# Sums of six second-weight slices moved to later steps, and DMA issue in program order with stores behind their data

## The chip, the cores and the metric

The kernel runs on one core of one Trainium2 chip. A core has TensorE (PE, matmuls, with weight loads shown apart as PEld), VectorE (DVE), ScalarE (ACT), GpSimd (POOL) and SyncE (SP), which here issues every DMA; 16 DMA engines serve the core. The metric is the device time of one execution in microseconds (us), as a median over runs.

## What is computed

```python
attn  = concat([softmax(scale * x @ state.T) @ state,         # per batch and head
                softmax(scale * state @ x.T) @ x], axis=2)    # 4 x 8 heads, 512 + 32 rows, 64 columns
x     = attn.transpose(0, 2, 1, 3).reshape(2176, 512)   # all tokens, 512 columns
h     = x @ w_in                                              # 512 -> 2048
x     = (maximum(h, 0) + alpha * minimum(h, 0)) @ w_out       # 2048 -> 512

P = exp(x @ w_gate - max)                                     # 8 experts
for _ in range(8):
    P /= P.sum(1, keepdims=True) + 1e-9
    P /= P.sum(0, keepdims=True) + 1e-9
    P *= N / E
out = sum over e of P[:, e:e+1] * (maximum(x @ w1[e], 0) @ w2[e])   # w1[e]: 512 x 1024, w2[e]: 1024 x 512
```

Everything is float32. Each product is made of three matmuls: an operand is split into a high part in the matmul's own format and a low part (the rest), and high by low, high by high and low by high are added up.

## The kernel before

The program has a first part (attention and the dense layer, to about 440 us) and the expert part, the function `experts`, which the change touches.

The weights of the 8 experts are cut into 32 slices (`U2 = 32`, four of 256 hidden columns for each expert). The tokens are cut into three groups, so the expert part has `NS2 = 96` steps: step s works on slice s % 32 for group s // 32. A product with the first weights is made by seven multiplications of blocks in place of eight (`quad`, with the banks x, y and z in PSUM); for this each slice's matrix of first weights needs four sums of its blocks, made on GpSimd (`weights_a`). In steps 32 to 95 the product with the second weights is made in the same way (`product`), and needs four sums of the second weights' blocks. In steps 0 to 31 the second product is made plainly (`layer2_moe`, tile `po`), without those sums.

Steps 0 to 31 therefore prepare the weights for all later ones. For a slice, the first weights (tiles `wah`, `wal`, and the sums `wsh`, `wsl`) and the second weights (`w2h`, `w2l`, and the sums, tile `wz`) are made once from the raw weights, and stored to DRAM (`keep`). From step 32 on they are loaded back (`again`) and nothing of them is worked out again. The sums of the second weights are `sums_left` on DVE (four operations of 128x256 into the tile `sumb`), a copy of each pair on ACT into the high half of `wz`, and one DVE subtraction of 128x512 for each low half: six DVE and two ACT operations for a slice, all in the step of that slice (`weights_b`). The tile `wz` has one or two homes, so the next slice's copy waits until the store of this one has read it.

What is written in which order: `experts` emits a step as seven multiplications and, in steps 1 to 32, six plain second products between them. After each it calls `slot()`, 13 times in a full step. A slot lets each lane (a queue of generators: weights, gate, sums and so on) go one yield further, and fires the entries of the list `soon` that are due. DVE, ACT and PE run their instructions in exactly this written order; for SP a scheduler chose the order. Each engine works through its own queue in order, and an instruction that waits holds all those behind it.

In steps 0 to 4 the gate is also under way: after the logits (`pg`) the eight rounds of normalization (`sinkhorn`, L449 to L464) run as a chain. In a round DVE does nine small operations (`rs`, `pr`, `cs`, `cb`), PE sums over the partitions with a matmul (`pcs`) and DVE goes on from it. The rounds are written five slots apart, and `pcs` stands in PE's queue between the multiplications.

Of the kernel before, what the change touches and what calls it, by code (L numbers as in the profile page):

```python
# [19 lines left out]
P = 128  # L20
# [24 lines left out]
def body(ctx: ExitStack, tc: tile.TileContext, xt_in, xn_in, stb, stk, wd, ws, alpha, wgate, out):  # L45
# [630 lines left out]
    def keep(u, what, tiles, i):  # L676

        for x, t in zip("hl", tiles, strict=True):
            if (u, what, x) not in kept:
                kept[u, what, x] = dram.tile([P, 7, FU], F32, tag=f"{what}{x}{u}", name=f"kept_{what}{x}{u}")  # L680
            nc.sync.dma_start(out=kept[u, what, x][:, i:i + t.shape[1], :], in_=f32(t))

    def again(u, what, tiles, i):

        for x, t in zip("hl", tiles, strict=True):
            nc.sync.dma_start(out=f32(t), in_=kept[u, what, x][:, i:i + t.shape[1], :])
# [19 lines left out]
    def weights_a(s):  # L706
# [6 lines left out]
        if s >= U2:  # L713
            again(u, "a", wa, 0)
            again(u, "a", wsum, 3)
            return
# [8 lines left out]
        keep(u, "a", wa, 0)  # L725
# [4 lines left out]
        keep(u, "a", wsum, 3)  # L730
# [4 lines left out]
    def weights_b(s):  # L735
# [8 lines left out]
        if s >= U2:  # L744
            pairs = []
            for i in range(2):
# [4 lines left out]
                pairs.append([z[:, j] for j in range(2)])  # L751
            w = [x.rearrange("p f (b c) -> p (f b) c", c=FU)[:, 0:3] for x in w]
            name_left(left2, s, w, pairs)
            again(u, "b", w, 0)
            again(u, "b", pairs[0], 3)
            again(u, "b", pairs[1], 5)
# [8 lines left out]
        keep(u, "b", [x[:, 0:1, 0:FU] for x in w], 0)  # L765
        keep(u, "b", [x[:, 1].rearrange("p (b c) -> p b c", c=FU) for x in w], 1)
# [5 lines left out]
        halves = raw.rearrange("p f (b c) -> p f b c", c=FU)  # L772
        yield from sums_left(nc.vector, sums, halves[:, 0, 0], halves[:, 1, 0], halves[:, 1, 1], halves[:, 0, 1], 1)
        load_b2(s + 1, p2["raw"])
        for i in range(2):
            if i and s >= 2 and s != U2 - 1:
                z = big.tile([P, 2, 2, FU], F32R, tag="xl3" if s < U2 - 6 else "xl5", name=f"wz_{s}_{i}")
            else:
                z = p2["z"].tile([P, 2, 2, FU], F32R, tag="z", name=f"wz_{s}_{i}", bufs=1)
# [581 lines left out]
    def experts():  # L1361
# [132 lines left out]
```

## Time and profile before

| | |
|---|---|
| three timed runs | 1876.51, 1880.92 and 1881.73 us; median 1880.92 |
| the profiled execution | 1878.26 us, span 1876.4 us |
| PE | 1793.8 us busy (96%) |
| DVE | 1495.2 us (80%) |
| POOL | 1259.6 us (67%) |
| ACT | 736.2 us (39%) |
| DMA | 424.09 MB, mean 226 GB/s |

The span is from the first to the last instruction of the program. A busy PE is a PE with a matmul in it; at half of its clock it is busy for twice as long with the same work, so its granted clock (PEclk, a share of 2.4 GHz) is read with it. In the expert part a step takes 15.6 us where nothing disturbs it in the first group, 14.6 us in the second and 12.3 us in the third.

### The profile page before, as it was taken

Reading aid. Unit: us, or ns where it says so; the run is one execution under the profiler, and the core shown is the slowest. Engines: PE = TensorE matmul, PEld = TensorE weight load, DVE = VectorE, ACT = ScalarE, POOL = GpSimd, SP = SyncE. Lnnn points to the kernel's source line nnn. Section 1 sums busy time; section 2 is a strip of 40 time slices with the busy share of each in tenths; the row PEclk is TensorE's granted clock in tenths of the full one; section 3 lists DMA queues with packets and bytes.
Section 4 is the critical chain, followed back from the end, with each engine's and each line's share of the span. In section 5 each row is a group of like instructions: output and inputs, shape, how many; then the busy total and the mean of one; then the engine's idle time right before and its main releaser. Section 6 shows DMA issues by size and latency. Waiting matters only on the chain.

```text
span 1876.4 us, 29641 instructions
## 1 busy us (share of the span) xinstructions
PE 1793.8 (96%) x10173; PEld 1667.3 (89%) x10173; DVE 1495.2 (80%) x2318; ACT 736.2 (39%) x1394; POOL 1259.6 (67%) x1297
## 2 busy tenths in 40 slices
PE   6799999988989999999999999999999999999998
PEld 5688888876778888888889999999999999999997
DVE  6744777776899998988997777777788888777886
ACT  6755666644333434333332222222223233332332
POOL 4523555465657877778756777777777898777774
PEclk8899999999999999999999999999999999999998
DMA  5111111122658888888788777777777788888882
GB/s 219 46 51 46 57 46 57 46 73 110 236 209 290 311 303 298 296 299 312 276 310 315 253 255 263 263 265 250 257 267 252 273 306 306 314 312 312 299 300 88
DMA packets 179525, 424.09 MB, mean 226 GB/s; under 512 B 20256, under 2 KB 37152, under 8 KB 179376
## 3 DMA queue, kind: packets, MB, share of 16 engines
q1 hardware_dynamic: 179376, 422.20, 63.4%
q8 instruction: 81, 1.33, 0.3%
q14 instruction: 68, 0.56, 0.1%
HBM read 299.13 MB, written 122.99 MB: 225 GB/s over the span
## 4 chain that ended last, share of the span: by engine, by line
PE 67%; DVE 6%; DMA 1%; issue 1%; ACT 0%; SPq 0%; DVEq 0%; ACTq 0%
PE pm L989 22%; PE py L816 14%; PE po L1133 11%; PE px L816 9%; PE pz L816 9%; DMA kept_bl<-wz 1%; DVE g2l L839 1%; DVE wz L784 1%; DVE oa L1151 0%; DVE c L823 0%; PE pe L1065 0%; DVE u L823 0%; DVE m L995 0%; DMA wsl<-kept_al 0%; DVE oa L1155 0%
## 5 line engine op out<-in xcount | busy, mean ns | idle before, releaser
L995 DVE TENSOR_TENSOR m<-pm,m 128x768 f32<-128x768 f32 (+1 forms) x427 | 378.0, 887 | 124.1 <-PE pm L989 124.1
L989 PE MATMUL pm<-formgh,wz 128*128 128x384 f32 (+1 forms) x1134 | 212.6, 322 | 0.3 <-DVE m L995 0.3
L920 POOL TENSOR_TENSOR formgh<-mid,formgh 128x384 fp32r<-128x384 f32 (+1 forms) x126 | 121.4, 964 | 107.9 <-ACT formgh L919 107.8
L816 PE MATMUL py<-rT,wsh 128*128 128x384 f32 (+1 forms) x768 | 189.3, 329 | 1.8 <-DVE u L823 1.7
L816 PE MATMUL px<-rB,wah 128*128 128x384 f32 (+1 forms) x768 | 189.2, 329 | 1.1 <-DVE g2l L839 1.0
L989 PEld LDWEIGHTS pm<-formgh,wz 128*128 128x128 f32 x1134 | 186.7, 188 | 0.6 <-issue 0.6
L536 POOL TENSOR_TENSOR gl<-r,gh 128x512 fp32r<-128x512 f32 (+1 forms) x80 | 94.4, 1192 | 114.8 <-ACT gh L535 60.2
L838 ACT ACTIVATE g2h<-c 128x384 fp32r<-128x384 f32 x96 | 50.5, 526 | 301.9 <-DVE c L823 301.9
L672 POOL TENSOR_TENSOR w2l<-rw,w2h 128x512 fp32r<-128x512 f32 x64 | 86.0, 1366 | 115.9 <-ACT w2h L670 95.8
L1133 PE MATMUL po<-w2l,g2h 128*128 128x512 f32 x384 | 153.4, 399 | 0.0
L1133 PE MATMUL po<-w2h,g2l 128*128 128x512 f32 x384 | 150.8, 393 | 2.6 <-DVE g2l L839 2.6
L1133 PE MATMUL po<-w2h,g2h 128*128 128x512 f32 x384 | 152.5, 397 | 0.0
L816 PEld LDWEIGHTS px<-rB,wah 128*128 128x128 f32 x768 | 136.7, 189 | 7.9 <-DVE g2l L839 1.8
L816 PEld LDWEIGHTS py<-rT,wsh 128*128 128x128 f32 x768 | 136.8, 190 | 6.0 <-DVE u L823 2.6
L930 POOL TENSOR_TENSOR T<-mid,mid 128x384 f32<-128x384 f32 (+1 forms) x126 | 118.3, 963 | 31.2 <-DVE mid L904 30.8
L1155 DVE SCALAR_TENSOR_TENSOR oa<-po,pr,oa 128x512 f32<-128x512 f32 x168 | 124.4, 741 | 16.9 <-PE po L1133 16.2
L919 ACT ACTIVATE formgh<-mid 128x384 fp32r<-128x384 f32 (+1 forms) x126 | 63.0, 500 | 177.8 <-DVE mid L904 131.0
L551 PE MATMUL po<-gl,wh 128*128 128x512 f32 (+1 forms) x320 | 120.1, 376 | 13.0 <-DVE acc L568 11.2
L904 DVE SCALAR_TENSOR_TENSOR mid<-mid,pb 128x384 f32<-128x384 f32 (+1 forms) x192 | 121.9, 635 | 6.6
L816 PE MATMUL py<-rT,wsl 128*128 128x384 f32 (+1 forms) x384 | 125.7, 327 | 0.0
L816 PE MATMUL px<-rB,wal 128*128 128x384 f32 (+1 forms) x384 | 125.6, 327 | 0.0
L823 DVE TENSOR_TENSOR u<-py,p 128x384 f32<-128x384 f32 (+1 forms) x192 | 102.3, 533 | 28.4 <-PE py L816 16.7
(255 smaller groups left out, 5187.7 us busy)
## 6 DMA issues: line engine op xcount, KB each, us to landing
wsh<-kept_ah SPq DMA_DIRECT2D x64, 512.0 KB, 4.0
wsl<-kept_al SPq DMA_DIRECT2D x64, 512.0 KB, 5.2
wz<-kept_bh SPq DMA_DIRECT2D x126, 256.0 KB, 5.9
wz<-kept_bl SPq DMA_DIRECT2D x126, 256.0 KB, 5.9
wah<-kept_ah SPq DMA_DIRECT2D x64, 384.0 KB, 3.0
wal<-kept_al SPq DMA_DIRECT2D x64, 384.0 KB, 3.7
w2h<-kept_bh SPq DMA_DIRECT2D x63, 384.0 KB, 5.8
w2l<-kept_bl SPq DMA_DIRECT2D x63, 384.0 KB, 6.6
```

The lines of the kernel that those rows point to most:

```text
L536: nc.gpsimd.tensor_tensor(out=lo, in0=r, in1=f32(hi), op=ALU.subtract)
L551: nc.tensor.matmul(ps, lhsT=w2(wt, u, f, d * P, P), rhs=g[:, f, :n], start=(i == 0), stop=(i == 3 * NF - 1))
L672: nc.gpsimd.tensor_tensor(out=lo[:, i], in0=src[:, i], in1=f32(hi[:, i]), op=ALU.subtract)
L816: nc.tensor.matmul(bank[b], lhsT=w[:, k * P:(k + 1) * P], rhs=xf[:, j, k, :], start=(first and i == 0), stop=(i == 5), skip_group_check=True,)
L823: nc.vector.tensor_tensor(out=out, in0=bank[b], in1=t[x], op=ALU.add)
L904: nc.vector.scalar_tensor_tensor(out=out, in0=src, scalar=0.0, in1=pb[:, e % 2, h * n:(h + 1) * n], op0=ALU.max, op1=ALU.mult)
L920: nc.gpsimd.tensor_tensor(out=lo, in0=out, in1=f32(hi), op=ALU.subtract)
L930: nc.gpsimd.tensor_tensor(out=out, in0=x, in1=y, op=ALU.subtract)
L989: nc.tensor.matmul(ps[:, q, :n], lhsT=w[:, q * P:(q + 1) * P], rhs=x, start=(j == 0), stop=(j == 2))
L995: nc.vector.tensor_tensor(out=mm[g][name], in0=ps[:, :, :n], in1=mm[g][name], op=ALU.add)
L1133: nc.tensor.matmul(ps, lhsT=x[:, f, t * P:(t + 1) * P], rhs=w[:, f, :], start=(i == 0), stop=(i == 3 * NF - 1))
L1155: nc.vector.scalar_tensor_tensor(out=a, in0=ps, scalar=p, in1=a, op0=ALU.mult, op1=ALU.add)
```

## The change

Five things are edited.

1. The sums of the second weights are taken out of the steps of slices 0, 1, 2, 3, 4 and 31 (`APART`). A new lane, `apart`, which starts in step 6, loads these six raw slices a second time, one after the other, and makes their sums then, in homes of their own (`rwl` in xh4, `sumb` in xl4, `wz` in xl5). A slice takes 34 slots: the additions stand at slots 0, 2, 3 and 5, the copies of ACT at 6 and 20 and the subtractions of DVE at 7 and 21. The first addition stands at slot 16 from the start of step 6, which is in step 7, and the last subtraction in step 21.
2. In the steps of these six slices the next raw slice is loaded one slot after the split and not after the sums.
3. `keep` no longer issues a store at once: it puts it on `soon`, to be written into the program three slots later.
4. The kept tensors are cut by what is stored together, so that each is one DMA: the high and low half of a `wz` are one store and one load of 512 KB, where they were two of 256 KB.
5. SP joins the engines whose order is the written order (`manual_schedule`) in the expert part, and the load of the routing weights `pb` is written in the middle of a step and not ahead of it.

The instructions of PE are the same, in the same order. DVE and ACT have the same instructions apart from those that are moved; there are six loads more (3 MB).

```diff
-    def keep(u, what, tiles, i):
-        for x, t in zip("hl", tiles, strict=True):
...
-            nc.sync.dma_start(out=kept[u, what, x][:, i:i + t.shape[1], :], in_=f32(t))
+    def keep(key, i, n, src):
+        if key not in kept:
...
+        soon.append([3, lambda: nc.sync.dma_start(out=kept[key][:, i:i + src.shape[1], :], in_=f32(src))])
+    def again(key, t):
+        nc.sync.dma_start(out=f32(t), in_=kept[key])
...
+        if s in APART:
+            load_b2(s + 1, p2["raw"])
+            yield 1
+            return
         yield 2
-        if s < 2:
-            sums = p2["t"].tile([P, 4, FU], F32, tag="y", name=f"sumb{s}", bufs=1)
...
+        yield from sums_b(u, raw, "xh5", 1, 0)
+
+    def sums_b(u, raw, home, gap, rest):
+        sums = big.tile([P, 4, FU], F32, tag=home, name=f"sumb{u}")
+        halves = raw.rearrange("p f (b c) -> p f b c", c=FU)
+        yield from sums_left(
+            nc.vector, sums, halves[:, 0, 0], halves[:, 1, 0], halves[:, 1, 1], halves[:, 0, 1], gap
+        )
+        if not rest:
+            load_b2(u + 1, p2["raw"])
         else:
-            sums = big.tile([P, 4, FU], F32, tag="xh5", name=f"sumb{s}")
...
+            load_apart(u)
         for i in range(2):
...
             nc.scalar.activation(out=hi, in_=src, func=AF.Copy)
             yield 1
             nc.vector.tensor_tensor(out=lo, in0=src, in1=f32(hi), op=ALU.subtract)
-            keep(u, "b", (hi, lo), 3 + 2 * i)
-            yield 1
+            keep(("bs", i, u), 0, 4, z.rearrange("p x b c -> p (x b) c"))
+            yield 1 + rest
+
+    APART = [0, 1, 2, 3, 4, U2 - 1]
...
+    def load_apart(u):
+        i = APART.index(u) + 1 if u is not None else 0
+        if i < len(APART):
+            v = APART[i]
+            raw_apart[v] = big.tile([P, NF, DM], F32, tag="xh4", name=f"rwl_{v}")
+            nc.sync.dma_start(out=raw_apart[v], in_=ws[v, 1].rearrange("p (f c) -> p f c", f=NF))
+
+    def apart():
+        load_apart(None)
+        yield 16
+        for u in APART:
+            yield from sums_b(u, raw_apart[u], "xl4", 2, 12)
...
+            if s == UE + 2:
+                lanes["apart"].append(apart())
...
+            if s == U2 - 6:
+                flush("apart")
...
-        with tc.manual_schedule(engines={mybir.EngineType.DVE}):
+        with tc.manual_schedule(engines={mybir.EngineType.DVE, mybir.EngineType.SP}):
             experts()
```

What stands in DVE's queue between step 0 and step 1, before the change (`c` and `g2l` are the results of step 0's multiplications, `u` the first add of step 1):

```order
L823 TENSOR_TENSOR c_0_4183<-pz_4069,u_0_4053 128x384
L695 TENSOR_TENSOR sumb_4197<-rw_0_4006 128x256
L698 TENSOR_TENSOR sumb_4197<-sumb_4197,rw_0_4006 128x256
L700 TENSOR_TENSOR sumb_4197<-rw_0_4006 128x256
L703 TENSOR_TENSOR sumb_4197<-rw_0_4006,sumb_4197 128x256
L784 TENSOR_TENSOR wz_0_4204<-sumb_4197,wz_0_4204 128x512
L784 TENSOR_TENSOR wz_1_4209<-sumb_4197,wz_1_4209 128x512
L823 TENSOR_TENSOR u_1_4239<-py_4232,p_1_4223 128x384
L839 SCALAR_TENSOR_TENSOR g2l_4015<-c_0_4104,g2h_4014 128x384
L839 SCALAR_TENSOR_TENSOR g2l_4015<-px_4016,g2h_4014 128x384
```

And after it:

```order
L857 TENSOR_TENSOR c_0_4183<-pz_4069,u_0_4055 128x384
L857 TENSOR_TENSOR u_1_4222<-py_4215,p_1_4206 128x384
L873 SCALAR_TENSOR_TENSOR g2l_4017<-c_0_4104,g2h_4016 128x384
L873 SCALAR_TENSOR_TENSOR g2l_4017<-px_4018,g2h_4016 128x384
L873 SCALAR_TENSOR_TENSOR g2l_4017<-c_0_4154,g2h_4016 128x384
```

The six operations on slice 0 are gone from between `c` and `u`.

DVE's queue in step 7 after the change (`rw_7` is that step's own raw slice, `rwl` the raw slice 0 that is loaded again):

```order
L693 TENSOR_TENSOR sumb_5370<-rw_7_5254 128x256
L696 TENSOR_TENSOR sumb_5370<-sumb_5370,rw_7_5254 128x256
L693 TENSOR_TENSOR sumb_5383<-rwl_5169 128x256
L1189 SCALAR_TENSOR_TENSOR oa_4288<-po_6_1_5385,pr,oa_4288 128x512
L698 TENSOR_TENSOR sumb_5370<-rw_7_5254 128x256
L857 TENSOR_TENSOR u_7_5413<-py_5345,p_7_5328 128x384
L857 TENSOR_TENSOR c_7_5415<-pz_5372,u_7_5413 128x384
L701 TENSOR_TENSOR sumb_5370<-rw_7_5254,sumb_5370 128x256
L696 TENSOR_TENSOR sumb_5383<-sumb_5383,rwl_5169 128x256
L1189 SCALAR_TENSOR_TENSOR oa_4288<-po_6_2_5422,pr,oa_4288 128x512
L873 SCALAR_TENSOR_TENSOR g2l_5320<-c_7_5415,g2h_5319 128x384
L698 TENSOR_TENSOR sumb_5383<-rwl_5169 128x256
```

The rows with `rwl` are new in this step; all others stood there before in the same order.

SP's queue for the stores of one step and the loads for the next, before:

```order
L681 DMA kept_ah_5247<-wah_5216 128x768
L681 DMA kept_al_5249<-wal_5217 128x768
L681 DMA kept_ah_5247<-wsh_5218 128x1024
L681 DMA kept_al_5249<-wsl_5219 128x1024
L665 DMA rw_7_5313<-in_ws_dram 128x1024
L681 DMA kept_bh_5228<-wz_0_5315 128x512
L681 DMA kept_bl_5230<-wz_0_5315 128x512
```

And after:

```order
L681 DMA kept_a_h_5184<-wah_5155 128x768
L681 DMA kept_a_l_5185<-wal_5156 128x768
L665 DMA rw_7_5254<-in_ws_dram 128x1024
L681 DMA kept_as_h_5224<-wsh_5157 128x1024
L681 DMA kept_as_l_5225<-wsl_5158 128x1024
L681 DMA kept_bs_6_5266<-wz_0_5256 128x1024
```

The load of the next raw slice (L665) now stands ahead of the two stores of `wsh` and `wsl`, and a `wz` is stored by one DMA.

## Rows read from the trace of the kernel before

**Rows 1.** Busy time by stretch: PE, PEld, DVE, ACT, POOL, then PEclk, DMA share, GB/s.
```profile
440.21:491.50 51.29, 43.53 (x227) 35.97 (x226) 32.56 (x63) 20.21 (x36) 24.06 (x28) 0.93 0.51 190
491.50:548.80 57.30, 45.25 (x208) 38.31 (x207) 54.81 (x123) 15.81 (x29) 34.91 (x40) 0.94 0.68 243
569.60:866.80 297.20, 297.20 (x1488) 266.54 (x1488) 271.75 (x404) 120.17 (x215) 234.50 (x247) 1.00 0.84 299
900.00:962.80 62.80, 62.77 (x314) 56.10 (x313) 62.56 (x92) 24.62 (x44) 46.08 (x48) 1.00 0.80 291
962.80:997.20 34.40, 31.30 (x152) 26.80 (x151) 30.16 (x43) 11.94 (x20) 11.52 (x9) 1.00 0.88 317
1466.50:1839.30 372.80, 372.80 (x2547) 372.29 (x2546) 304.70 (x482) 115.25 (x246) 296.98 (x338) 1.00 0.85 303
```

**Rows 2.** Waits at 440.21 to 548.8 us: total us, times, longest us.
```profile
ACT wz L782 <- DMA kept_bl<-wz: 11.4, 2, 6.1
...
PE pcs L459 <- DVE cs L456: 11.1, 5, 3.8
...
PE pz L816 <- DVE g2l L839: 7.6, 1, 7.6
```

**Rows 3.** Order of time on DVE around 460 us; idle before it in brackets.
```profile
458.48 1.75 DVE L784 TENSOR_TENSOR wz<-sumb,wz 128x512 fp32r<-128x512 f32 x1
463.88 0.69 DVE L784 TENSOR_TENSOR wz<-sumb,wz 128x512 fp32r<-128x512 f32 x1 [3.65 <-ACT wz L782]
464.49 0.55 DVE L823 TENSOR_TENSOR u<-py,p 128x384 f32<-128x384 f32 x1
...
466.24 1.61 DVE L839 SCALAR_TENSOR_TENSOR g2l<-c,g2h 128x384 fp32r<-128x384 f32 x2
```

**Rows 4.** DVE groups at 491.5 to 548.8 us: busy us, mean ns of one.
```profile
L784 DVE TENSOR_TENSOR wz<-sumb,wz 128x512 fp32r<-128x512 f32 x6 | 5.3, 886 | 0.0
...
L695 DVE TENSOR_TENSOR sumb<-rw 128x256 f32<-128x256 f32 x3 | 2.0, 670 | 0.0
...
L698 DVE TENSOR_TENSOR sumb<-sumb,rw 128x256 f32<-128x256 f32 x3 | 3.1, 1029 | 0.1
...
L700 DVE TENSOR_TENSOR sumb<-rw 128x256 f32<-128x256 f32 x3 | 1.7, 579 | 0.0
...
L703 DVE TENSOR_TENSOR sumb<-rw,sumb 128x256 f32<-128x256 f32 x3 | 1.6, 537 | 0.0
```

**Rows 5.** The same groups at 569.6 to 866.8 us, 19 steps.
```profile
L784 DVE TENSOR_TENSOR wz<-sumb,wz 128x512 fp32r<-128x512 f32 x38 | 44.6, 1174 | 0.0
...
L698 DVE TENSOR_TENSOR sumb<-sumb,rw 128x256 f32<-128x256 f32 x19 | 20.7, 1087 | 0.7
...
L695 DVE TENSOR_TENSOR sumb<-rw 128x256 f32<-128x256 f32 x19 | 18.4, 970 | 0.0
...
L700 DVE TENSOR_TENSOR sumb<-rw 128x256 f32<-128x256 f32 x19 | 18.1, 953 | 0.0
...
L703 DVE TENSOR_TENSOR sumb<-rw,sumb 128x256 f32<-128x256 f32 x19 | 11.5, 603 | 0.0
```

**Rows 6.** Order of time: one operation with GpSimd idle, one with it at work.
```profile
456.36 0.42 DVE L698 TENSOR_TENSOR sumb<-sumb,rw 128x256 f32<-128x256 f32 x1
...
695.01 2.55 POOL L672 TENSOR_TENSOR w2l<-rw,w2h 128x512 fp32r<-128x512 f32 x2 [3.19 <-DMA kept_bh<-wz]
...
696.59 1.25 DVE L695 TENSOR_TENSOR sumb<-rw 128x256 f32<-128x256 f32 x1
```

**Rows 7.** Order of time on ACT in step 31.
```profile
979.83 0.63 ACT L782 ACTIVATE wz<-sumb 128x512 fp32r<-128x512 f32 x1 [3.88 <-DMA kept_bl<-wz]
```

**Rows 8.** A load's issue, the operation that reads it, its usual time to landing.
```profile
704.01 0.71 SPq L665 DMA_DIRECT2D rw<-in_ws_dram  x1
...
709.52 1.05 ACT L670 ACTIVATE w2h<-rw 128x1024 fp32r<-128x1024 f32 x1
...
rw<-in_ws_dram SPq DMA_DIRECT2D x19, 512.0 KB, 4.7
```

More of the change, by code (lines that the diff above doesn't have):

```diff
@@ L674, in body @@
     kept = {}
[L676 to L686 removed]
+    def keep(key, i, n, src):
+        if key not in kept:
+            name = "kept_" + "_".join(map(str, key))
+            kept[key] = dram.tile([P, n, FU], F32, tag=name, name=name)
+        soon.append([3, lambda: nc.sync.dma_start(out=kept[key][:, i:i + src.shape[1], :], in_=f32(src))])
+    def again(key, t):
+        nc.sync.dma_start(out=f32(t), in_=kept[key])
     def name_left(into, s, base, pairs):
@@ L713, in weights_a @@
         if s >= U2:
-            again(u, "a", wa, 0)
-            again(u, "a", wsum, 3)
+            for x, w, t in zip("hl", wa, wsum, strict=True):
+                again(("a", x, u), w)
+                again(("as", x, u), t)
             return
@@ L724, in weights_a @@
         split2(*wa, t[:, 0:3, :])
-        keep(u, "a", wa, 0)
+        for x, w in zip("hl", wa, strict=True):
+            keep(("a", x, u), 0, 3, w)
         yield next(make) + 1
@@ L729, in weights_a @@
         split2(*pairs[1], sums[:, 2:4, :])
-        keep(u, "a", wsum, 3)
+        for x, w in zip("hl", wsum, strict=True):
+            keep(("as", x, u), 0, 4, w)
         if "raw" in p2:
@@ L764, in weights_b @@
                 nc.sync.dma_start(out=whole[x], in_=f32(t))
-        keep(u, "b", [x[:, 0:1, 0:FU] for x in w], 0)
-        keep(u, "b", [x[:, 1].rearrange("p (b c) -> p b c", c=FU) for x in w], 1)
-        yield 2
-        if s < 2:
-            sums = p2["t"].tile([P, 4, FU], F32, tag="y", name=f"sumb{s}", bufs=1)
-        else:
-            sums = big.tile([P, 4, FU], F32, tag="xh5", name=f"sumb{s}")
-        halves = raw.rearrange("p f (b c) -> p f b c", c=FU)
-        yield from sums_left(nc.vector, sums, halves[:, 0, 0], halves[:, 1, 0], halves[:, 1, 1], halves[:, 0, 1], 1)
-        load_b2(s + 1, p2["raw"])
+        for x, t in zip("hl", w, strict=True):
+            keep(("b", x, u), 0, 3, t[:, 0:1, 0:FU])
+            keep(("b", x, u), 1, 3, t[:, 1].rearrange("p (b c) -> p b c", c=FU))
+        if s in APART:
+            load_b2(s + 1, p2["raw"])
+            yield 1
+            return
+        yield 2
+        yield from sums_b(u, raw, "xh5", 1, 0)
[7 more added lines that the diff above has]
+            load_b2(u + 1, p2["raw"])
+        else:
+            load_apart(u)
         for i in range(2):
-            if i and s >= 2 and s != U2 - 1:
-                z = big.tile([P, 2, 2, FU], F32R, tag="xl3" if s < U2 - 6 else "xl5", name=f"wz_{s}_{i}")
+            if rest:
+                z = big.tile([P, 2, 2, FU], F32R, tag="xl5", name=f"wz_{u}_{i}")
+            elif i:
+                z = big.tile([P, 2, 2, FU], F32R, tag="xl3" if u < U2 - 6 else "xl5", name=f"wz_{u}_{i}")
             else:
-                z = p2["z"].tile([P, 2, 2, FU], F32R, tag="z", name=f"wz_{s}_{i}", bufs=1)
+                z = p2["z"].tile([P, 2, 2, FU], F32R, tag="z", name=f"wz_{u}_{i}", bufs=1)
             hi, lo = z[:, 0], z[:, 1]
@@ L1178, in body @@
     made = {}
-    later, soon, lanes = [], [], {"x": [], "state": [], "gate": [], "early": [], "sums": [], "blocks": [], "v": [], "w": [], "w2": [], "h": [], "out": []}
+    later, soon, lanes = [], [], {"x": [], "state": [], "gate": [], "early": [], "sums": [], "blocks": [], "v": [], "w": [], "w2": [], "apart": [], "h": [], "out": []}
     wait = dict.fromkeys(lanes, 0)
```

19 lines of the change are left out of this document (11 added, 8 removed).

## The prediction

> **What bounds the kernel now.** I read the busy time by stretch first. In steps 6 to 24 (569.60 to 866.80 us) PE is busy for all of 297.20 us, and in 30 steps of the third group (1466.50 to 1839.30 us) for all of 372.80 us; both run at a granted clock of 1.00, the upper level of 2.4 GHz [rows 1]. PE's instructions stay the same in the same order, so these two stretches can only lose. Time can come back only where PE has holes, and the same view shows three such stretches: 440.21 to 491.50 us (steps 0 to 2), 491.50 to 548.80 us (the eight rounds of normalization) and 962.80 to 997.20 us (steps 31 and 32). PE is busy there for 43.53 of 51.29, 45.25 of 57.30 and 31.30 of 34.40 us [rows 1]. These are the steps that lose their own sums.
>
> The waits tell who is late. In the first stretch PE waits once, for 7.6 us, for DVE's `g2l`; ACT's `wz` copy has waited 11.4 us in two goes for the store of the `wz` before it [rows 2]. DVE in order of time shows the link: the second subtraction of slice 0 starts only at 463.88, after 3.65 us in which DVE waited for that copy, and `u` and the `g2l` that PE wants are queued right behind it [rows 3]. So store, copy, subtraction, `g2l` and PE form one chain. In the second stretch PE waits for the small operations of the rounds (`pcs` for `cs`, 11.1 us in five goes) [rows 2], and DVE is busy for 54.81 of 57.30 us [rows 1]: the rounds are late because DVE is full.
>
> **Steps 0 to 2.** The change takes the six operations out from between `c` and `u`. What is left is PE's own work. The granted clock of 0.93 means that about 0.14 of 51.29 us, 7.2 us, ran at the lower level of 1.2 GHz (the two levels average to 0.93); at the upper level this work takes half, 3.6 us less. So PE needs 43.53 - 3.6 = 39.9 us, and 51.29 - 39.9 = 11.4 could go. I take off 1 us for hand-offs which were hidden behind the wait: **10.4**. The low bound is 6.8, if the clock stays as it was (51.29 - 43.53 = 7.8, less the same 1).
>
> **The normalization.** Three slices lie in this stretch, and their sums take DVE 5.3 + 2.0 + 3.1 + 1.7 + 1.6 = 13.7 us [rows 4]. Without them DVE needs 54.81 - 13.7 = 41.1. PE needs 45.25 less half of the time at the lower clock (0.94, so 0.12 x 57.30 = 6.9, half is 3.4): 41.8. The two come out almost level, so neither hides the other's hand-offs; each of the eight rounds passes from DVE to PE and back, and I put 0.4 us on each, 3 us, by choice. 41.8 + 3 = 44.8, a gain of **12.5**. Bounds: 15.5 with no such loss, and 4 if the chain of a round, and not DVE's fullness, sets its pace (then about a third of the 11.1 us of `pcs` waits goes).
>
> **Steps 31 and 32.** In step 31 ACT's copy waited 3.88 us for a store [rows 7]. Slice 31's sums go, PE needs its 31.30 us at full clock, and 34.40 - 31.30 = **3.1** comes back; at least 1, if a load of step 32 is late next.
>
> **Where the work goes.** The new lane puts 6 x 6 = 36 operations on DVE, 24 additions and 12 subtractions, into steps 7 to 21: 15 steps. PE has no hole there, so all depends on DVE's room. DVE is busy for 271.75 of 297.20 us over 19 steps [rows 1], so it is idle for 25.45 / 19 = 1.34 us in a step and 20.1 us in 15 steps. Another stretch shows that this room can be used up: at 900.00 to 962.80 us DVE is busy for 62.56 of 62.80 us and PE loses nothing [rows 1].
>
> The price of one operation is what the trace leaves open. With GpSimd idle, a 128x256 addition took 0.42 us; another began while GpSimd was in two `w2l` subtractions and took 1.25 us, ending near the end of these [rows 6]. A 128x512 subtraction took 1.75 us and 0.69 us [rows 3]. This gives three prices for a slice. All uncontended: 4 x 0.42 + 2 x 0.69 = 3.06, so 18.4 us for six slices, inside the 20.1 us of room: cost nothing. The means of the normalization stretch: 0.670 + 1.029 + 0.579 + 0.537 + 2 x 0.886 = 4.59 [rows 4], so 27.5, an excess of 7.4. The means of steps 6 to 24: 1.087 + 0.970 + 0.953 + 0.603 + 2 x 1.174 = 5.96 [rows 5], so 35.8, an excess of 15.7. GpSimd is busy for 234.50 of 297.20 us, 79% [rows 1], and by their slots I count 25 of the 36 operations beside its work: 25/36 x 35.8 + 11/36 x 18.4 = 30.5, an excess of 10.4. Some of it stays a backlog which steps 22 and 23, without a moved slice, take up (2 x 1.34 = 2.7, say 2.4 of it). I take **8** as the cost, with 0 and 15.7 as bounds.
>
> The Trainium skill ("SBUF — State Buffer", section "Who interferes with whom") says that a VectorE instruction with two inputs in SBUF and a GpSimd instruction that reads SBUF hold one shared port as an exclusive lock, and that the loser blocks for the whole instruction. The addition of 1.25 us beside the one of 0.42 us agrees with it [rows 6]. By that rule taken to its end, every moved operation waits out one whole GpSimd instruction.
>
> **What I cost at nothing.** ACT's twelve moved copies: ACT is busy for 120.17 of 297.20 us [rows 1]. DMA: six loads and six slices' stores move into or are added to steps 7 to 21. Their traffic goes from 299 GB/s x 297.20 us / 19 = 4.68 MB in a step to about 5.28 (0.5 MB read and 1 MB stored again for 6 slices, 9 MB over 15 steps), so the DMA share of 0.84 goes to about 0.95 (an estimate in proportion). The next raw load is issued at 704.01, its first reader runs at 709.52, and such a load takes 4.7 us: 5.5 - 4.7 = 0.8 us to spare [rows 8]. The written order issues it ahead of the `wsh` and `wsl` stores, which were ahead of it, and so covers a slower transfer; were the cover gone, it would cost up to 1 us a step. Stores written three slots later meet data that are ready, so SP stands less, and only homes that wait for a store come free later; the moved sums have homes of their own. In the third group a step's loads will stand together near its start; at the DMA share of 0.85 [rows 1] they fill about 0.85 x 372.80 / 30 = 10.6 us of a step's 12.4, and the next step needs them, the sums not before its third multiplication.
>
> **Sum.** 1878.26 - 10.4 - 12.5 - 3.1 + 8 = 1860.3 for the profiled execution. The median of the three runs is 1880.92, 2.7 above it, so the forecast is **1862 us**.
>
> **Rivals**, as the median. (a) The moved operations are nearly free: then all 26 to 30 us come back, 1851 to 1855. For it speaks that two operations of six in a slice stand where GpSimd rests; against it the means in rows 5, which already are those of these steps. (b) DVE becomes the bound in steps 7 to 21 at those means: 26.0 - 15.7 = 10.3 saved, 1871. PE then has holes behind `c`, `u` and `g2l`. For it speaks a DVE that is 91% busy (271.75 of 297.20). (c) The rounds are a chain whatever else DVE does: 26.0 - 12.5 + 4 - 8 = 9.5 saved, 1871. Against it: DVE has next to no idle time in that stretch. (d) The fuller queue makes the raw load late in each of the 15 steps by 1 us: 1862 + 15 = 1877, no measurable change. (e) Slower: DVE's additions and subtractions wait for GpSimd at every turn. It decides the sign where the moved operations take more than 26.0 + 20.1 = 46.1 us together (1.28 us each), and it is measurably slower from 51.7 us (1.44 each). At the highest prices that I show, 24 x 1.25 + 12 x 1.75 = 51.0 [rows 3, 6], an excess of 30.9: 1881 - 26.0 + 30.9 = 1886, the edge of it. If each waited for two operations of GpSimd together (2.55) half of the time, 36 x 1.28 + 18.4 = 64.5, an excess of 44.4 and 1899. Against it: the means in rows 5 are far below, at 0.60 to 1.17 us. The rule of the Trainium skill named above leads to the latter number, and the trace bears it out for single operations only.
>
> **How the numbers follow.** About 0.3%, 5.6 us, is what a measurement of this kernel can tell from no change, so "same" is 1875 to 1887. The chances: the forecast (1856 to 1870) 0.55; (a) 0.13; (b) 0.09; (c) 0.06; (d) 0.08; (e) 0.09. Faster is the forecast with (a), (b) and (c): 0.83. Same is (d) and 0.02 of (e), whose price may fall near 46 us: 0.10. Slower is the rest of (e): 0.07. The range from **1850 to 1877 us** holds all cases but (e) and half of (d), 0.13 left out. Its low end is all gains at no cost (11.4 + 15.5 + 3.1 = 30.0 saved, 1851); its high end is the low bounds of the first and third gain at the highest price of rows 5 (6.8 + 12.5 + 1 - 15.7 = 4.6 saved, 1876).
>
> **What would show it.** After the change PE's hole before 466 us is gone, and ACT has no `wz` wait for a store in steps 0 to 4 and 31. The 108.6 us of the first two stretches become about 86, at a granted clock near 1.00, and `pcs` waits fall from 11.1 to 3 us or less. Steps 31 and 32 take 31.3 us. In steps 7 to 21 DVE is 98% busy or more, PE has small holes which sum to about 8 us and end at `c`, `u` or `g2l`; the moved additions show a mean near 0.8 us. PE stays full at 1466 to 1839 us. The prediction is wrong if the holes in steps 7 to 21 sum to over 16 us, if they end at `w2h` or another operation that waits for a load (then the DMA queue, and not DVE, is the price), if the rounds keep their pace, or if later steps wait for loads.

## The result, and the profile after

The changed kernel takes 1863.28 us (median of four runs, 1858.33 to 1865.91), the kernel before 1878.72 us beside it: a ratio of 0.9912, with a 95% interval of 0.9894 to 0.9929. So it is 0.9% faster; the forecast was 1862 us.

PE's records are the same 10173 in the same order in both traces, so each stretch of before can be found again in the trace after by its first and last PE instruction. The busy time by stretch after the change, for steps 0 to 2, the normalization, steps 6 to 24, steps 31 and 32, and the long stretch of the third group, as in [rows 1]:

```profile
440.30:482.60 42.30, 41.56 (x227) 34.44 (x226) 28.54 (x53) 18.42 (x33) 29.07 (x33) 1.00 0.56 199
482.60:528.20 45.60, 41.27 (x207) 35.96 (x206) 42.55 (x103) 12.39 (x22) 27.05 (x34) 1.00 0.57 208
549.20:854.80 305.60, 300.32 (x1487) 265.55 (x1486) 300.69 (x439) 123.56 (x226) 233.66 (x247) 1.00 0.90 324
951.20:981.60 30.40, 30.40 (x153) 27.24 (x152) 25.40 (x37) 10.90 (x18) 11.26 (x9) 1.00 0.91 334
1450.90:1825.70 374.80, 373.25 (x2547) 372.24 (x2545) 305.85 (x482) 114.96 (x246) 296.30 (x338) 1.00 0.83 304
```

The first two stretches are down from 51.29 and 57.30 us to 42.30 and 45.60, and PE's clock there is at its upper level all the time (1.00, where it was 0.93 and 0.94). Steps 31 and 32 went from 34.40 to 30.40 us. The price stands in the third row: 305.60 us for the 297.20 of before, with DVE busy for 300.69 of them. PE's holes there are 5.28 us; the other 3 us of the loss stand in PE's busy time, 300.32 us for 297.20 with the same instructions at the same clock, so a PE that waits is in part counted as busy. The last row holds a loss that the prediction did not have: 374.80 us for 372.80.

PE's waits for the rounds and for `g2l` at 440.3 to 552 us, beside those of [rows 2] (total us, times, longest us):

```profile
PE pcs L459 <- DVE cs L456: 4.3, 3, 2.6
...
PE pz L850 <- DVE g2l L873: 0.6, 1, 0.6
```

The `pcs` waits are down from 11.1 to 4.3 us (3 or less was expected), and the one of 7.6 us for `g2l` to 0.6. The copy `wz` no longer waits here, since it is not made here. The new waits, in steps 6 to 24 (weight loads, PEld, shown apart from matmuls):

```profile
PEld px L850 <- DVE g2l L873: 5.4, 6, 1.6
...
PEld py L850 <- DVE u L857: 3.4, 4, 1.7
PE px L850 <- DVE g2l L873: 2.9, 4, 1.1
...
PE py L850 <- DVE u L857: 1.9, 3, 1.2
```

They end where the prediction said they would, at DVE's `g2l` and `u`. No PE wait ends at a load.

The ledger below is worked out so: for each pair of PE instructions that bound a stretch, the time between them in the run's trace less the time between the same two in the trace of before. The part of the program ahead of the expert part is the same in all kernels and differs by up to 9 us between profiled executions, so it stays out. Three more parts are left out: the stretch between the normalization and step 6 (-0.8 to +0.6 us, and -2.4 with only wsh, wsl late), the second group (0.1 us at most either way) and the end of the program behind the third group's stretch (0.1 to 1.7 us less than before, and 4.0 less with the scheduler's SP order). Each row is read from one execution, so a difference of 1 or 2 us between two rows can be chance. Times and ratios are from timed runs, each ratio beside runs of the kernel before on the same chip. The names in the first column are explained with the experiments.

| run | median, us | ratio to before, 95% interval | steps 0-2 | normalization | steps 6-24 | steps 25-30 | steps 31-32 | third group |
|---|---|---|---|---|---|---|---|---|
| the change | 1863.3 | 0.9912 (0.9894 to 0.9929) | -9.0 | -11.7 | +8.6 | +0.4 | -4.1 | +2.1 |
| nothing moved | 1875.4 | 0.9979 (0.9968 to 0.9990) | -1.5 | -2.7 | 0.0 | -0.9 | +1.4 | +0.8 |
| moved, no DVE work | 1858.1 | 0.9879 (0.9862 to 0.9896) | -9.0 | -11.1 | 0.0 | -0.4 | -4.1 | +3.7 |
| moving alone | 1923.8 | 1.0232 (1.0216 to 1.0248) | -9.0 | -11.1 | +56.5 | +13.4 | -4.1 | 0.0 |
| stores at once | 1941.6 | 1.0326 (1.0310 to 1.0341) | -8.1 | -9.8 | +58.8 | +23.0 | -2.6 | +1.1 |
| spread | 1861.0 | 0.9894 (0.9873 to 0.9915) | -9.0 | -11.2 | +7.8 | -1.3 | -4.1 | +3.5 |
| quiet place | 1857.2 | 0.9868 (0.9846 to 0.9891) | -9.0 | -11.6 | 0.0 | -0.5 | -4.1 | +2.1 |
| joined alone | 1875.6 | 0.9978 (0.9963 to 0.9994) | -1.6 | -3.4 | 0.0 | -1.1 | +0.1 | 0.0 |
| scheduler's SP order | 1858.2 | 0.9870 (0.9849 to 0.9892) | -9.0 | -11.6 | +5.6 | -1.6 | -4.1 | +0.4 |
| quiet place, scheduler's SP order | 1852.1 | 0.9844 (0.9817 to 0.9870) | -9.0 | -11.4 | 0.0 | -1.7 | -4.1 | 0.0 |
| only wsh, wsl late | 1860.2 | 0.9874 (0.9849 to 0.9900) | -9.0 | -10.6 | +7.0 | -0.5 | -4.1 | +2.0 |
| loud place | 1870.1 | 0.9941 (0.9918 to 0.9964) | -9.0 | -11.7 | +13.7 | +2.5 | -4.1 | +0.7 |
| joined, homes of before | 1883.7 | 1.0009 (0.9996 to 1.0022) | +2.5 | 0.0 | 0.0 | -0.9 | +2.8 | +0.1 |

### The profile page after: what moved, and what is told of

Its sections match the earlier page's. It is cut to its first block, busy times and chain, and to the rows that moved or that the text cites. A ratio compares the mean times of both kernels' runs of the same rounds, so it can differ in the third digit from the quotient of the medians.

```text
span 1862.5 us, 29291 instructions
## 1 busy us (share of the span) xinstructions
PE 1791.9 (96%) x10173; PEld 1662.6 (89%) x10173; DVE 1507.0 (81%) x2318; ACT 732.8 (39%) x1394; POOL 1252.4 (67%) x1297
## 4 chain that ended last, share of the span: by engine, by line
PE 69%; DVE 16%; POOL 4%; issue 4%; DMA 3%; ACT 3%; SPq 1%; DVEq 0%; POOLq 0%; ACTq 0%
PE pm L1023 22%; PE py L850 11%; PE px L850 8%; PE pz L850 8%; PE po L551 7%; PE po L1167 5%; PE ph L522 4%; DVE oa L1189 2%; DVE wz L800 2%; DVE g2l L873 1%; POOL w2l L672 1%; DMA kept_bs<-wz 1%; PE pv L484 1%; DVE c L857 1%; DMA rw<-in_ws_dram 1%
## 5 line engine op out<-in xcount | busy, mean ns | idle before, releaser
L1023 PE MATMUL pm<-formgl,w2h 128*128 128x384 f32 (+1 forms) x504 | 121.2, 323 | 3.4 <-DVE m L1029 1.9
```

The source lines that it names most:

```text
L1023: nc.tensor.matmul(ps[:, q, :n], lhsT=w[:, q * P:(q + 1) * P], rhs=x, start=(j == 0), stop=(j == 2))
```

## The experiments

### What the lost time in steps 6 to 24 is made of

**Moved, no DVE work.** The lane loads and stores as before, but DVE does nothing in it; ACT copies both halves of each `wz` from the raw slice, for the two halves i of it 14 slots apart:

```diff
+    def bare_b(u, raw):
...
+            nc.scalar.activation(out=z[:, 0], in_=src, func=AF.Copy)
+            yield 1
+            nc.scalar.activation(out=z[:, 1], in_=src, func=AF.Copy)
+            keep(("bs", i, u), 0, 4, z.rearrange("p x b c -> p (x b) c"))
...
-            yield from sums_b(u, raw_apart[u], "xl4", 2, 12)
+            yield from bare_b(u, raw_apart[u])
```

> The new lane does everything but its DVE work: the raw slices are loaded again, ACT makes both halves of each wz as copies of the raw slice, and the stores are as they were. So the sums of six slices of the second weights are left out, and all of the DMA traffic stays. Theory (the lost 8.6 us of steps 7 to 21 are DVE's fullness): 1863.3 - 8.6 = 1854.7 us, PE without holes at 586 to 824 us. Rival (the loss is the DMA queue's, fuller by 3 MB and the moved stores): no gain, 1862 to 1864 us, with PE's holes still there and behind operations that wait for a load.

It took 1858.1 us, and the ledger shows 0.0 in steps 6 to 24 in place of 8.6, while the gains of the other stretches stayed. The whole price is DVE's; the six loads and the stores cost nothing there. The time came out 3 us above the 1854.7 expected. Of this the third group is 1.6 us (3.7 lost for 2.1) and the stretches from the normalization to step 6 are 1.0; the rest is not explained.

**Spread.** A slice takes 39 slots, so that the operations lie in 18 steps:

```diff
-            yield 1 + rest
+            yield 1 + rest + (1 if rest and i else 0)
...
-            yield from sums_b(u, raw_apart[u], "xl4", 2, 12)
+            yield from sums_b(u, raw_apart[u], "xl4", 2, 14)
```

> The same 36 operations on DVE, a slice in 39 slots in place of 34, so that they lie in 18 steps (7 to 24) and not in 15. Theory (DVE's room is what is short): three steps more give 3 x 1.34 = 4.0 us more of it, the loss of 8.6 us becomes about 4.6, and the time 1859 us for 1863. Rival (each moved operation that meets GpSimd's work costs PE by itself, however much room there is): the loss stays, 1863 us.

The loss was 7.8 us, and not 4.6: the theory as it stood failed in its number. The time, 1861.0 us, lies between those of the theory and its rival and decides nothing.

**Quiet place.** Two operations in each of the same 18 steps, between the last `g2l` of a step and the first `u` of the next (`low` is the subtraction of a half, `high` its copy on ACT, `make` the four additions):

```diff
-        yield 16
+        yield 12
...
         for u in APART:
-            yield from sums_b(u, raw_apart[u], "xl4", 2, 12)
+            if last:
+                low(*last)
+            yield 1
...
+            next(make)
+            yield 12
+            next(make)
+            yield 1
+            next(make)
+            yield 10
+            last = high(u, 0, sums)
+            yield 2
+            next(make)
+            load_apart(u)
+            yield 1
+            low(*last)
+            yield 10
+            last = high(u, 1, sums)
+            yield 2
+        low(*last)
```

> The same 36 operations in the same 18 steps, two in each, written between the last g2l of a step and the first u of the next, where GpSimd has nothing to do for about 3 us of each step. Theory (an operation is dear because GpSimd works beside it): 3.06 us for a slice, 18.4 us in all for 18 x 1.34 = 24.1 us of room, so the loss of 8.6 us goes and the time is 1855 us; the moved additions take 0.45 us and the moved subtractions 0.7 us. Rival (the room alone counts): as with the operations spread over 18 steps, 1859 us.

It took 1857.2 us, between the 1855 of the theory and the 1859 of the rival; the prices and the ledger decide, below.

**Loud place.** The quiet place's kernel, with the lane begun six slots later:

```diff
-        yield 12
+        yield 18
...
         for u in APART:
```

> The same pattern as at the quiet place, two operations in each of 18 steps, but six slots later, in the middle of GpSimd's work. Theory (GpSimd's work beside them makes them dear): the moved additions take 0.8 to 1.2 us and the subtractions 1.1 us or more, as a slice 5.3 to 6 us, so 32 to 36 us for 24.1 us of room, and 8 to 12 us are lost in steps 7 to 24: 1863 to 1867 us. Rival (it was the even spread of two in each step that made them free): 1857 us, as at the quiet place.

It took 1870.1 us, above the 1863 to 1867 expected: the moved operations took 37.4 us and not 32 to 36, and 2.5 us more went in steps 25 to 30.

The moved operations at the quiet place (busy us, mean ns of one; L827 are the moved subtractions):

```profile
L827 DVE TENSOR_TENSOR wz<-sumb,wz 128x512 fp32r<-128x512 f32 x12 | 8.2, 685 | 0.0
L693 DVE TENSOR_TENSOR sumb<-rwl 128x256 f32<-128x256 f32 x6 | 2.5, 424 | 0.2
L701 DVE TENSOR_TENSOR sumb<-rwl,sumb 128x256 f32<-128x256 f32 x6 | 2.5, 419 | 0.0
L698 DVE TENSOR_TENSOR sumb<-rwl 128x256 f32<-128x256 f32 x6 | 2.5, 418 | 0.0
L696 DVE TENSOR_TENSOR sumb<-sumb,rwl 128x256 f32<-128x256 f32 x6 | 2.5, 418 | 0.0
```

And at the loud place:

```profile
L827 DVE TENSOR_TENSOR wz<-sumb,wz 128x512 fp32r<-128x512 f32 x12 | 14.4, 1203 | 0.2 <-ACT wz L823 0.2
...
L696 DVE TENSOR_TENSOR sumb<-sumb,rwl 128x256 f32<-128x256 f32 x6 | 5.8, 962 | 0.0
L701 DVE TENSOR_TENSOR sumb<-rwl,sumb 128x256 f32<-128x256 f32 x6 | 5.8, 959 | 0.0
L698 DVE TENSOR_TENSOR sumb<-rwl 128x256 f32<-128x256 f32 x6 | 5.7, 956 | 0.0
L693 DVE TENSOR_TENSOR sumb<-rwl 128x256 f32<-128x256 f32 x6 | 5.7, 956 | 0.0
```

Nothing but the place differs, and the prices are 0.42 and 0.69 us at the one, 0.96 and 1.20 us at the other. In steps 6 to 24 this is 0.0 us lost against 13.7.

The place could stand for something other than GpSimd. ACT it is not: at the quiet place ACT works all through each of the 24 additions, and at the loud place all through 12 of them and not at all beside the other 12, which take 0.96 us either way. GpSimd's part can be read for each operation, here one of the loud place and one of the changed kernel (start, us):

```profile
638.01 0.93 POOL L693 TENSOR_TENSOR sum<-rw 128x256 f32<-128x256 f32 x1
...
638.27 0.95 DVE L698 TENSOR_TENSOR sumb<-rwl 128x256 f32<-128x256 f32 x1
```

```profile
578.55 0.73 POOL L701 TENSOR_TENSOR sum<-rw,sum 128x256 f32<-128x256 f32 x1
...
578.94 0.62 DVE L701 TENSOR_TENSOR sumb<-rwl,sumb 128x256 f32<-128x256 f32 x1
```

GpSimd's instructions end at 638.94 and 579.28, the additions beside them 0.28 us later, at 639.22 and 579.56. So it is with all 65 moved additions of the changed kernel, the spread and the loud run that began while a GpSimd instruction ran: each ended 0.28 to 0.29 us after that instruction. The 31 of the changed kernel and the quiet place that began with GpSimd idle took 0.41 to 0.43 us. So the price of an addition is what is left of one GpSimd instruction, and 0.28 us.

PE at the quiet place, in the stretch of steps 6 to 24:

```profile
553.50:850.60 297.10, 297.10 (x1488) 266.50 (x1487) 284.96 (x439) 125.58 (x226) 231.33 (x247) 1.00 0.90 330
```

It is busy for all of 297.10 us, as before the change, and DVE for 284.96.

Do these prices and the room of 1.34 us in a step give the losses? Loud: 5.8 + 5.8 + 5.7 + 5.7 + 14.4 = 37.4 us, less 18 x 1.34 = 24.1, is 13.3 (13.7 measured, with 2.5 more by step 30). Quiet: 10.0 + 8.2 = 18.2, which fits in 24.1 (0.0). In the changed kernel the additions take (at 564 to 810 us):

```profile
L698 DVE TENSOR_TENSOR sumb<-rwl 128x256 f32<-128x256 f32 x6 | 5.6, 932 | 0.0
L701 DVE TENSOR_TENSOR sumb<-rwl,sumb 128x256 f32<-128x256 f32 x6 | 4.7, 786 | 0.0
L693 DVE TENSOR_TENSOR sumb<-rwl 128x256 f32<-128x256 f32 x6 | 4.7, 777 | 0.0
L696 DVE TENSOR_TENSOR sumb<-sumb,rwl 128x256 f32<-128x256 f32 x6 | 4.2, 705 | 0.0
```

These are 19.2 us. The twelve subtractions share a line with those of the steps' own slices; told apart by their place in DVE's written order they take 0.67 to 1.38 us, 11.9 in all. That is 31.1 us, less 20.1 of room 11.0, of which 8.6 showed; steps 22 to 24 have room for up to 4.0. In the spread run the additions took 21.0 us (0.96 for three of the four) and the subtractions 0.67 to 0.69 each, 8.2: 29.2 in all, less 24.1, is 5.1, and 7.8 were lost. There the sum doesn't come out. It leaves out that moved operations push the steps' own ones into other places. The spread run has for two of the steps' own additions (at 554 to 850 us, 19 steps):

```profile
L696 DVE TENSOR_TENSOR sumb<-sumb,rw 128x256 f32<-128x256 f32 x19 | 26.6, 1400 | 0.6
L693 DVE TENSOR_TENSOR sumb<-rw 128x256 f32<-128x256 f32 x19 | 23.9, 1260 | 0.0
```

Before it was 20.7 and 18.4 us for the same two [rows 5]. So the runs show what makes a moved operation dear, and that at the price with GpSimd idle it costs nothing; by which rule the price turns into lost time they leave open. The rival of the spread run stands: beyond the 18.2 us of the quiet place the operations took 12.9 us in the change, 11.0 in the spread and 19.2 in the loud run, and 8.6, 7.8 and 13.7 were lost, 0.67 to 0.71 of it each time, whatever the room.

The Trainium skill ("SBUF — State Buffer", section "Who interferes with whom") has VectorE with two SBUF inputs and a GpSimd instruction that reads SBUF exclude each other for a whole instruction. The traces agree: an addition that meets a GpSimd instruction ends only behind it. They don't bear out the worst case that the prediction drew from it (64.5 us for the 36 operations, with a whole instruction of 1.28 us waited out by each); the loud place comes to 37.4, where an addition met the last 0.67 to 0.68 us of an instruction.

### What the written order and the later stores do

**Moving alone** undoes edit 3 and SP's part of edit 5, and keeps the joined transfers:

```diff
-        with tc.manual_schedule(engines={mybir.EngineType.DVE, mybir.EngineType.SP}):
+        with tc.manual_schedule(engines={mybir.EngineType.DVE}):
...
-        soon.append([3, lambda: nc.sync.dma_start(out=kept[key][:, i:i + src.shape[1], :], in_=f32(src))])
+        nc.sync.dma_start(out=kept[key][:, i:i + src.shape[1], :], in_=f32(src))
```

> The moving alone: SP's order is again the scheduler's choice, and stores are issued at once; the joined transfers stay. Theory: the written order is worth nothing in the first group, so 1863 us as with the whole change, or 1861 if the hole of 1.5 us at 1594 us, where an output store stood behind eight loads, goes with it. Rival (the order by the scheduler puts stores ahead of loads, and the moved sums need the written order): 1870 us or more, with DVE or GpSimd waiting for raw loads in steps 7 to 21.

**Stores at once** undoes edit 3 alone (the second pair of lines above).

> SP keeps the written order, but a store is written where its data are written, and not three slots later, so SP stands at every store until its data are there, and the loads behind it stand too. Theory (SP's standing is hidden, as the prediction priced it at nothing): 1863 us. Rival (the raw loads have 0.8 us to spare, and lose 1 us or more in each of some 25 steps): 1885 us or more, with GpSimd and ACT waiting for raw loads.

Both rivals were right by far: 1923.8 and 1941.6 us, slower than the kernel before. The gains of steps 0 to 5 are there in both, and 56 to 59 us go in steps 6 to 24, 3 us a step, and 13 to 23 more by step 30. The waits of the moving alone at 620 to 870 us:

```profile
POOL sum L693 <- DMA rw<-in_ws_dram: 86.0, 13, 7.5
ACT w2h L670 <- DMA rw<-in_ws_dram: 68.1, 13, 6.9
DVE sumb L693 <- DMA rw<-in_ws_dram: 40.3, 12, 4.8
```

GpSimd waits 6.6 us for the raw loads, 13 times in 250 us. SP in order of time over one such step (L656 to L665 are the four raw loads):

```profile
691.07 0.32 SPq L681 DMA_DIRECT2D kept_as_l<-wsl  x1
...
710.26 0.32 SPq L681 DMA_DIRECT2D kept_as_l<-wsl  x1
710.63 0.42 SPq L656 DMA_DIRECT2D rw<-in_ws_dram  x1
711.11 0.72 SPq L657 DMA_DIRECT2D rw<-in_ws_dram  x1
711.87 0.47 SPq L658 DMA_DIRECT2D rw<-in_ws_dram  x1
712.39 0.45 SPq L665 DMA_DIRECT2D rw<-in_ws_dram  x1
```

GpSimd and ACT in the same step:

```profile
706.33 3.90 POOL L672 TENSOR_TENSOR wsl<-sum,wsh 128x256 fp32r<-128x256 f32 x4
717.50 0.74 POOL L693 TENSOR_TENSOR sum<-rw 128x256 f32<-128x256 f32 x1 [7.26 <-DMA rw<-in_ws_dram]
```

```profile
718.60 1.06 ACT L670 ACTIVATE w2h<-rw 128x1024 fp32r<-128x1024 f32 x1 [4.25 <-DMA rw<-in_ws_dram]
```

This is a ring. GpSimd makes `wsl` until 710.2; SP has stood for that and issues the store at 710.26, and only then the four loads that it has behind it (710.63 to 712.39); GpSimd's next step begins when they are in, at 717.50, and ACT's at 718.60. Once around takes 710.26 - 691.07 = 19.2 us, against 15.6 for PE's work. In the kernel before the three small loads stood ahead of the next step's stores (691.69 to 693.49 us there), and only L665 behind the `wsl` store, with its 0.8 us to spare [rows 8]. So they stand in the run with joined transfers alone too (below); with the moved sums in the program the scheduler put all four behind. The Trainium skill ("DMA: Bandwidth & Descriptors", section "Anatomy of one DMA — SWDGE (gpsimd) path") says, of DMA engines in general, that a wait on a semaphore is held by the sequencer that issues the DMA. SP's standing here agrees with that: the four loads go out in the 2.6 us right behind the store. That the stores of `wsh` and `wsl` are what holds them is tested next.

**Only wsh, wsl late** tests the ring: the written order with stores at once, but for two stores of a step:

```diff
         soon.append([3, lambda: nc.sync.dma_start(out=kept[key][:, i:i + src.shape[1], :], in_=f32(src))])
+        if key[0] != "as":
+            soon.pop()[1]()
```

> SP's written order and stores at once, as in the run that was 60 us slower, but for the two stores of wsh and wsl, which are written three slots later. Theory (the slow runs are a ring: a raw load waits on SP behind the wsl store, that store waits for GpSimd's last operation of the step, and GpSimd's next step waits for the raw load): with these two stores out of the ring the steps come back to 15.6 us, and the time is near that of the whole change, 1861 to 1868 us. Rival (every store that SP meets before its data holds the loads up): 1885 us or more still.

1860.2 us: with these two stores out of the way the loss in steps 6 to 24 falls from 58.8 to 7.0 us. All the other stores may stand in front of their data at no cost that this run shows.

**Scheduler's SP order** undoes SP's part of edit 5 alone (the first pair of lines above).

> The whole change but SP's written order: the scheduler chooses it from a program in which stores stand three slots later. Theory (what counts is that no store stands ahead of a raw load before its data are there, and the place in the program gives the scheduler its order too): 1863 us as with the whole change. Rival (the scheduler puts the stores back ahead of the loads): 1900 us or more, with ACT and GpSimd waiting for raw loads in steps 9 to 30.

1858.2 us: the written order isn't needed once the stores are three slots later. In steps 6 to 24 this run lost 5.6 us, the one with only wsh and wsl late 7.0 and the whole change 8.6, with the moved operations at the same places in DVE's queue; one profile of each doesn't tell whether SP's order or chance makes that difference. Of the whole, the timed ratios suggest that the written order costs something: 0.9870 (0.9849 to 0.9892) without it and 0.9912 (0.9894 to 0.9929) with it, two intervals that just don't meet. In the third group this run lost 0.4 for 2.1, and that loss is seen in the changed kernel's SP (the first of eight loads, the last two, and an output store) and in ACT:

```profile
1578.78 0.38 SPq L684 DMA_DIRECT2D wah<-kept_a_h  x1
...
1581.80 1.07 SPq L684 DMA_DIRECT2D wz<-kept_bs  x2
1582.96 0.49 SPq L1053 DMA_DIRECT2D out_dram<-row  x1
```

```profile
1592.21 0.60 ACT L1077 ACTIVATE row<-pt 128x512 f32<-128x512 f32 x1 [5.52 <-DMA out_dram<-row]
```

The store is issued at 1582.96, right behind loads that began at 1578.78, and ACT can write its buffer again only at 1592.21, after a wait of 5.52 us; 1.5 us of it reach PE at 1594 us. The runs with SP's written order lose 0.7 to 3.7 us in the third group, those with the scheduler's 0.4 at most.

### What the rest of the change is worth

**Nothing moved** keeps everything but the moving:

```diff
-            elif i:
+            elif i and u != U2 - 1:
...
-    APART = [0, 1, 2, 3, 4, U2 - 1]
+    APART = []
```

> Nothing is set apart: each slice's sums stay in its own step, with the written order of SP, the stores three slots later and the joined transfers kept. Theory (all of the gain and of the cost is in the moved sums): the 24.7 us won in steps 0 to 5 and 31 and the 9.1 us lost in steps 6 to 30 both go, and the time is that of the kernel before, 1879 to 1882 us. In the trace ACT waits for the store of a wz in step 0 for 3 us or more, and the rounds of normalization take as long as before. Rival (the written order of SP and the later stores earn a part by themselves): 1872 us or less. Other rival (they cost by themselves, and the moving hides it): 1885 us or more.

**Joined alone** has the same edit and the two pairs of lines of the moving alone.

> Of the whole change only the joined transfers (and the load of the routing weights in mid-step) are kept: nothing is set apart, SP's order is the scheduler's choice, stores are issued at once. It asks what made the moving without the written order 45 us slower in the expert part. Theory (the moved sums put GpSimd's work and with it the stores ahead of the raw load later, and the 0.8 us that this load has to spare are gone): without the moved sums the time is that of the kernel before, 1879 to 1881 us. Rival (one store of 512 KB for a wz in place of two of 256 KB takes the queue while the raw load is under way): 1900 us or more, with ACT and GpSimd waiting for raw loads.

Both came out 0.2% faster than before (1875.4 and 1875.6 us), with 4.3 and 4.9 us won in steps 0 to 2 and the normalization. But they have another difference from the kernel before. That kernel gave slices 0 and 1 one home for both `wz`, and `sumb` a home of its own; the changed `sums_b` has no such case, gives them two for `wz` and puts `sumb` elsewhere. DVE in order of time in the joined-alone run:

```profile
459.45 0.42 DVE L693 TENSOR_TENSOR sumb<-rw 128x256 f32<-128x256 f32 x1 [2.24 <-PE pg L375]
...
463.78 0.69 DVE L800 TENSOR_TENSOR wz<-sumb,wz 128x512 fp32r<-128x512 f32 x1 [0.15 <-ACT wz L798]
464.39 0.55 DVE L857 TENSOR_TENSOR u<-py,p 128x384 f32<-128x384 f32 x1
```

The 3.65 us that DVE stood for the copy [rows 3] are 0.15. In their place the first addition stands 2.24 us, as its new home was still read by PE's `pg`; so little is left: `u` comes at 464.39, 22.95 us behind the start of step 0's stretch (at 441.44 in this execution), where it was 24.28 before (464.49, with the start at 440.21).

**Joined, homes of before** puts the old homes back:

```diff
+        if u < 2:
+            sums = p2["t"].tile([P, 4, FU], F32, tag="y", name=f"sumb{u}", bufs=1)
...
-            elif i and u != U2 - 1:
+            elif i and u >= 2 and u != U2 - 1:
```

> Joined transfers alone, as in the run before with that name, but with the sums of slices 0 and 1 in the homes that the kernel before gives them (one home for both wz of a slice, sumb in a home of its own); that run had given them two homes for wz, since the changed function has no such case any more. Theory (the 5.0 us which that run won in steps 0 to 4 came from the second home: no wait of the wz copy for the store): nothing is won in steps 0 to 4, about 1 us at step 26 stays, and the time is 1878 us. Rival (one store of 512 KB is done sooner than two of 256 KB, and this shortens the wait): again 4 to 5 us won in steps 0 to 4, 1875 us.

Now the waits of [rows 2] are back, and the time is 1883.7 us, a ratio of 1.0009 (0.9996 to 1.0022):

```profile
ACT wz L801 <- DMA kept_bs<-wz: 12.0, 2, 6.6
...
PE pz L853 <- DVE g2l L876: 7.7, 1, 7.7
```

That is above the 1878 us expected, and by its interval no change from before. The joined transfers are worth 0.9 us in steps 25 to 30, and the profile shows more lost elsewhere: 2.5 us in steps 0 to 2, where the `wz` copy waits 12.0 us for 11.4 and PE's granted clock is 0.87 for 0.93, and 2.8 in steps 31 and 32. What the two runs above had won in steps 0 to 2 and the normalization came with the other homes.

### Both gains together

**Quiet place, scheduler's SP order** joins the edit of the quiet place with that of the scheduler's SP order.

> The moved operations at the quiet place, 18 steps, and SP's order left to the scheduler with the stores three slots later. Theory (the two gains are separate: the moved sums cost nothing there, and the output stores of the later groups are not held behind eight loads): in the expert part 24.7 us won in steps 0 to 5 and 31, 1.6 us at step 26, nothing lost in steps 6 to 24 and none of the 1.8 us in the third group, so 26 us ahead of the kernel before there and 1853 us. Rival (the scheduler's order moves with the program, and some raw load falls back behind GpSimd's last stores): 1870 us or more.

1852.1 us, a ratio of 0.9844 (0.9817 to 0.9870), the lowest of all, though its interval meets those of the quiet place and of the scheduler's SP order alone. Busy time in steps 6 to 24 and in the third group:

```profile
557.60:854.60 297.00, 297.00 (x1487) 266.46 (x1486) 284.49 (x438) 125.70 (x226) 229.95 (x247) 1.00 0.90 328
1448.70:1821.30 372.60, 372.60 (x2545) 372.10 (x2544) 304.45 (x482) 115.11 (x246) 296.23 (x338) 1.00 0.86 303
```

PE is full in both, and with +0.6 between the normalization and step 6 the parts sum to 25.6 us won, 26 expected (23.1 at the quiet place alone).

## Why the prediction was right, step by step

**Steps 0 to 2**: 10.4 us forecast, 9.0 measured, and 9.0 in eight other runs with these sums moved. The mechanism was right, a term mis-sized: PE's own work was taken as 39.9 us and is 41.56 us at full clock. The step that failed is that all of the time at the lower clock was counted as work of PE. The stretch at the lower level, in the trace of before:

```profile
463.36:470.19 6.83, 3.82 (x12) 3.70 (x12) 3.97 (x6) 1.91 (x4) 5.49 (x7) 0.50 0.48 181
```

PE is busy for 3.82 of these 6.83 us, and for the rest it still waits for `g2l`. So 1.9 us could go and not 3.6, and 43.53 - 1.9 = 41.6. **The normalization**: 12.5 forecast, 11.7 measured; PE's work came to 41.27 us (41.8 forecast) and the holes to 4.3 (3, put by choice). The chance given to a chain that keeps its pace whatever DVE does was not borne out. **Steps 31 and 32**: 3.1 forecast, 4.1 measured; PE is now busy for 30.40 us and not 31.30, so at the same clock of 1.00 part of the 31.30 can't have been its work; that PE waited there inside an instruction is likely and not shown.

**The cost in steps 7 to 21**: 8 forecast, 8.6 measured in steps 6 to 24. It is DVE's alone (0.0 without its operations), and it goes by GpSimd's work beside them (0.42 against 0.96 us for the same addition). The price was well put: 30.5 us forecast for the 36 operations, 31.1 measured, and 17 of 24 additions beside GpSimd where 25 of 36 operations had been counted. That the loss is what exceeds the room of 1.34 us a step holds at the two places (13.3 worked out, 13.7 measured; none at the quiet one) and not in the spread run (5.1 and 7.8), so this part of the mechanism stays open. The rival of nearly free operations needed only another place in the same queue.

**What was costed at nothing** is where the prediction was weak, though its sum did not suffer. The load's cover of 0.8 us was named, and its loss priced at 1 us a step; when the stores stand in front of the loads, the moved sums cost 3 us a step and more, since the ring then sets the pace of all steps to 30, and not only of those with moved work. The three slots between data and store are what keeps it off; SP's written order does not, and it loses 2.1 us in the third group, which had been put at 0. And the store of a `wz` was not the whole of the first chain: without its wait 1.6 of the 9.0 us came back, as another wait stood in for it.

The parts sum to -9.0 - 11.7 + 8.6 + 0.4 - 4.1 + 2.1 = -13.7 us, against 13.9 between the two profiled executions (1878.26 and 1864.35) and 18.0 forecast for them. So the terms hold 4 us too much gain, half of it the third group. That the forecast is within 1.3 us of the median all the same is in part luck. The forecast was to be raised by 2.7 us from the profiled execution to the median of three runs, which by its own sum gives 1863 and not 1862; and the median after lies 1.1 us below its profiled execution, where the median of three before lay 2.7 above. The gain in the medians is 15.4 us (1878.72 - 1863.28), of 18.9 forecast (1880.92 - 1862).

## What to carry to other kernels

Work that is moved into steps where PE is full has to be priced by its place and not by its mean: look for the stretch of each step in which the engine beside which they are dear, here GpSimd, rests, and write the moved operations there. Before a store is put into the queue that issues loads, ask what it waits for, and whether that is the last thing done with the previous load: then the two make a ring, and a few slots between data and store take it apart. And when an experiment leaves out a part, check that nothing else came with it: here the buffers of two slices did.

## What the runs showed of the hardware that was not expected

The same 128x256 addition on DVE takes 0.41 to 0.43 us when it begins with GpSimd idle (31 of 31), and one that begins while a GpSimd instruction runs ends 0.28 to 0.29 us after that instruction (65 of 65). At the loud place this makes 0.95 to 0.97 us for each, in the changed kernel 0.54 to 1.36. An output store of 256 KB, issued right behind eight loads on the same queue, held its buffer for 9.3 us (1582.96 to 1592.21). And one store of 512 KB in place of two of 256 KB gave nothing that the times show: 0.09% (-0.04 to +0.22).
